# Speech joint training kernel: the two ge-row tiles are cleared by VectorE at the start instead of by GpSimd after the first chunk

## The chip, the core and the metric

The kernel runs on one core of a Trainium2 chip. The metric is device time in microseconds (us), the median of several executions. Three executions of the kernel before took 789.6, 789.79 and 791.91 us; the median is 789.79 us.

## What is computed

The reference is the forward pass of a small speech network with a joint layer, followed by the gradients of all seven inputs. The forward pass, with B = 2 sequences, T = 16000 time steps, D = 256 channels, K = 3 taps and U = 8 label steps, is:

```python
h = sum over i in 0..2 of xp[:, i:i+T] @ w1[i]        # x padded by one at both ends
h = gelu(h)[:, ::2]
f = sum over i in 0..2 of hp[:, i:i+T1] @ w2[i]       # h padded by one at both ends
f = gelu(f)[:, ::2]                                   # 4000 rows for each sequence
fe = f @ w_f
ge = g @ w_g                                          # 8 rows for each sequence
j  = tanh(fe[:, :, None, :] + ge[:, None, :, :])      # B, 4000, 8, 256
out = j @ w_o
```

The outputs are `out` and, from a given `grad_out`, the gradients with respect to x, w1, w2, g, w_f, w_g and w_o. All tensors are bf16.

## The kernel before, in words

**Tiling.** The 2 x 4000 rows of `f` are taken as one row of 8000 columns and cut into 17 chunks: one of 256 columns, fifteen of 512 and a last one of 64. Channels lie on the 128 partitions, two tiles (kt) for 256 channels. For each chunk `stage_a` loads x transposed (XC), runs the two convolutions with their gelus (HTo, HTe, FT; `conv_gelu`, whose operations stand at L514 to L539, also makes the gelu's derivative factors G1o, G1e and G2 on VectorE) and FE. `stage_j` then goes over the eight label steps in four pairs: it makes `tanh(fe + ge)` (JT), the output rows (OUT_SB), and the gradient that flows back into the tanh (NGZ, added up in ZS). `stage_de` takes the gradient of the chunk before back through the convolutions and adds up the weight gradients (ACC).

**The ge rows.** In most chunks VectorE makes the tanh's argument a second time, row-wise: `JR = FER + GEB` at L686, with the rows on the partitions. This needs the eight `ge` rows of a sequence on every partition, the tile GEB, 128 x 2048 bf16, one tile for each sequence. `make_geb` (L606) fills it: GpSimd clears the tile (`memset`, L609), four DMAs from the GpSimd queue put the 8 x 256 values of `ge` (GER) on partitions 0, 32, 64 and 96 (issued at L363), and VectorE's `stream_shuffle` (L615) copies each of the four rows to its group of 32 partitions. In the source the shuffle has a planned delay of 45 us (first sequence) or 100 us (second). `ge_rows` makes GER from gT and WG on TensorE, with an evacuation on VectorE (L351). The first chunks do not use GEB: chunks 0 and 1 get JR by transposing JT on TensorE.

**Order of the work.** Nothing is issued in the order of the source. Each operation is recorded with its engine or engines, a planned cost, what it reads and writes, and a due time; `Flow.issue` then plays a list schedule through with the planned costs and emits each engine's instructions in the order that it found. Some evacuations may go to ScalarE or VectorE, as the schedule decides. A change of one operation's engine or cost can thus change the order, and the engine, of others far behind it. All loads and stores but a few go through SyncE's queue.

**The start.** VectorE clears a small tile (L1043), TensorE runs 20 matmuls on it to be busy, ScalarE loads its table. SyncE issues the first XC load, the weights W2, WF and WOT, and three GO loads; GpSimd makes `ident` and issues the two GR loads, later the WG and WO loads. Then chunk 0 is convolved, `make_ge` makes GE (L1077 transposes GR against `ident`; L1089 evacuates), and stage_j of chunk 0 begins with JT (L654) and the transposes of JT (L681).

Inside `conv_gelu`, on VectorE: L520 makes `g_s` from `g_sq` and the PSUM tile of the convolution, and so frees that PSUM tile; L531, L533, L535, L537 and L539 follow, of which L535 and L537 are `tensor_scalar` operations on bf16 tiles in SBUF. ScalarE's L529 (tanh of `g_s`) waits for both L520 of a convolution. There are seven PSUM tiles (`ps`) that all stages share.

Of the kernel before, what the change touches and what calls it, by code (L numbers as in the profile page):

```python
# [10 lines left out]
BF16 = mybir.dt.bfloat16  # L11
# [25 lines left out]
class Flow:  # L37
# [24 lines left out]
    def buf(self, cls, shape, dtype, name):  # L62
        b = Buf(cls, shape, dtype, name)
        s = self.seq[cls]
        b.seq, s[0] = s[0], s[0] + 1
        return b

    def op(self, eng, cost, fn, r=(), w=(), new=(), at=None, work=0.0, after=(), kind=None, behind=(), sub=None, lag=0.0):
        o = Op()
        o.eng = (eng,) if isinstance(eng, str) else tuple(eng)  # L70
        o.cost = cost if isinstance(cost, tuple) else (cost,) * len(o.eng)
        o.fn, o.new, o.work, o.n = fn, list(new), work, len(self.ops)
        o.prio = ((self.now if at is None else at) + self.shift.get((self.stage, sub), 0.0), o.n)
        o.succ, o.done, o.ready, o.kind, o.span, o.lag = [], None, 0.0, kind, None, lag
        deps, bufs = set(after), []
        for lst, wr in ((r, False), (w, True)):
            for x in lst:
                b, key = x if isinstance(x, tuple) else (x, None)
                for d, k, dw in b.log:
                    if (wr or dw) and (k is None or key is None or k == key):  # L80
                        deps.add(d)
                if b not in bufs:
                    bufs.append(b)
        for lst, wr in ((r, False), (w, True)):
            for x in lst:
                b, key = x if isinstance(x, tuple) else (x, None)
                if wr:
                    b.log = [e for e in b.log if not (key is None or e[1] == key)]
                b.log.append((o, key, wr))
        for b in o.new:  # L90
            b.born = o
        deps.discard(o)
        o.soft = ({b.born for b in bufs if b.born is not None} | set(behind)) - deps - {o}
        deps |= o.soft
        for b in o.new:
            if b not in bufs:
                bufs.append(b)
        o.deps, o.bufs = deps, bufs
        for b in bufs:
            b.users += 1  # L100
        o.left = len(deps)
        for d in deps:
            d.succ.append(o)
        self.ops.append(o)
        return o
# [110 lines left out]
def c_dve(n, f=1.0):  # L216
    return 66.0 + 1.042 * n * f
# [3 lines left out]
def kernel(  # L221
# [19 lines left out]
    nc = tc.nc  # L241
    B, T, D = x.shape
    KK = w1.shape[0]
    U = g.shape[1]
# [6 lines left out]
    P = 128  # L251
# [43 lines left out]
    op, buf = F.op, F.buf  # L295
# [9 lines left out]
    def fixed(shape, dtype, name, pool=None):  # L305
        b = Buf(None, shape, dtype, name)
        b.t = (pool or const).tile(shape, dtype, name=name)
        return b
# [14 lines left out]
    GER = fixed([U, B, D], BF16, "GER")  # L323
# [33 lines left out]
    def dma(q, out, in_, r, w, bytes_, new=(), transpose=False, at=None, after=(), cost=None, behind=(), sub="dma"):  # L357
        def go(e):
            eng_ = nc.sync if e == "SP" else nc.gpsimd if e == "POOL" else nc.scalar
            if transpose:  # L360
                eng_.dma_start_transpose(out=out(), in_=in_())
            else:
                eng_.dma_start(out=out(), in_=in_())  # L363
        c = cost or (1230.0 if transpose else 750.0 if q == "POOL" else 450.0)
        return op(q, c, go, r=r, w=w, new=new, at=at, after=after, behind=behind, sub=sub, kind="T" if transpose else "D",
                  work=bytes_ / 32768 * 165.0 if transpose else bytes_ / 304.0)
# [238 lines left out]

    def make_geb(b):  # L606

        GEB = buf("geb", [P, U, D], BF16, "GEB")
        op("POOL", 2100.0, lambda e: nc.gpsimd.memset(GEB[:], 0.0), r=[(GER, b)], w=[GEB], new=[GEB])  # L609
        for q in range(0, P, 32):  # L610
            dma("POOL", lambda q=q: GEB[q:q + 1], lambda: GER[:, b, :], r=[(GER, b)], w=[(GEB, q)], bytes_=4096)

        def spread(e):
            v = GEB[:].rearrange("p u d -> p (u d)").bitcast(FP32)
            nc.vector.stream_shuffle(v, v, [0] * 32)  # L615
        op("DVE", 66.0 + c_dve(U * D // 2), spread, r=[GEB], w=[GEB], sub="geb", lag=45000.0 if b == 0 else 100000.0)
        return GEB

    def mix_geb(G0, G1):
        px = [c.px for c in chunks if c.px is not None][0]  # L620
        GEB = buf("gx", [P, U, D], BF16, "GEB")
        op("DVE", c_dve(U * D, 0.25), lambda e: nc.vector.tensor_copy(out=GEB[:], in_=G1[:]), r=[G1], w=[GEB], new=[GEB])
# [378 lines left out]
    def gg_out():  # L1001
# [43 lines left out]
       r=[(warm, 0)], w=[(warm, 1)])  # L1045
# [4 lines left out]
            mm(wps[:, 0:2 * P], warm[:, 0, 0], warm[:, 0].rearrange("p k c -> p (k c)"), True, True)  # L1050
    op("PE", 20 * 215.0, warm_up, r=[(warm, 0)], w=[wps], new=[wps])
    op("POOL", 500.0, lambda e: make_identity(nc, ident[:]), w=[ident])

    def wload(q, dst, out, in_, n, at, after=()):
        return dma(q, out, in_, r=[], w=[dst], bytes_=n * 65536, at=at, cost=450.0 if q != "POOL" else 550.0, after=after)
# [48 lines left out]
    GEB = GEBX = None  # L1104
    for k in range(NG + 1):
# [15 lines left out]
        if k + 1 < NG and chunks[k + 1].px is not None:  # L1121
            F.now = t0 + Wk * 0.3
            GEB1 = make_geb(1)
            GEBX = mix_geb(GEB, GEB1)
        if k == 1:
            F.now = t0 + Wk * 0.1
            ge_rows()
            GEB = make_geb(0)
# [3 lines left out]
        if k < NG and c.px is not None:  # L1132
            GEB = GEB1
# [43 lines left out]
```

## Time and profile before

| what | us |
|---|---|
| median of three executions | 789.79 |
| the profiled execution, own time | 789.48 |
| its span, first to last instruction | 787.7 |
| PE (TensorE) busy | 770.0 |
| ACT (ScalarE) busy | 725.5 |
| DVE (VectorE) busy | 714.1 |
| POOL (GpSimd) busy | 96.2 |
| the two clears of GEB on POOL, each | 1.80 |
| the two shuffles of GEB on DVE, each (78.7 and 147.5 us) | 1.31 |

How to read the answers of the trace: times are us from the span's start. A timeline line has the start, the duration of the merged group, the engine, the line of the kernel, the operation, the tiles written and read, the size, and, in square brackets, how long the engine had been idle before it and which instruction ended that. An engine with a "q" behind its name is its sequencer, which issues DMAs. In a table of waits, each line names who waited for whom, the total in us, how often, and the longest. A line of busy time by window has, for each engine, busy us and the number of instructions, then the TensorE clock that was granted as a share of full speed, the busy share of the DMA engines and GB/s.

### The profile page before, as it was taken

To read this page: it belongs to the slowest core of one execution; us is meant where nothing else is said; L and a number is where in the kernel's file an instruction comes from. 1 tells how busy PE (TensorE), PEld (TensorE's weight loads), DVE (VectorE), ACT (ScalarE), POOL (GpSimd) and SP (SyncE) were. 2 spreads that over 40 slices of the span, in tenths; PEclk is the share of its full clock that TensorE was granted. 3 is DMA by queue.
4 is the path that set the end of the run, shared out by engine and by line. 5 is a ranking of instruction groups with operands and counts; after the bars stand their busy time and mean duration, and the time that the engine had idled before them with its cause. 6 is when DMAs were issued, how large, how long until landed. Compare 5 with 4: busy or idle time off the path is not lost. (4 is left out here: it accounts for less than half of the span.)

```text
span 787.7 us, 15636 instructions
## 1 busy us (share of the span) xinstructions
PE 770.0 (98%) x5668; PEld 533.6 (68%) x5668; DVE 714.1 (91%) x1503; ACT 725.5 (92%) x1178; POOL 96.2 (12%) x235
## 2 busy tenths in 40 slices
PE   6999999999999999999999999999999999999997
PEld 4657767576675767767677666676767767577775
DVE  5799999998998989989899898998989899899965
ACT  4999989999999999999999999999999999999833
POOL 4311110201102010020101101010020110203010
PEclk8999999999999999999999999999999999999999
DMA  9998999999999999999999999999998989989984
GB/s 212 175 208 187 232 252 244 238 240 243 222 227 227 266 232 215 233 257 225 229 211 244 243 230 226 214 257 219 229 252 203 264 209 227 248 225 239 229 204 144
DMA packets 382754, 178.86 MB, mean 227 GB/s; under 512 B 307762, under 2 KB 376468, under 8 KB 380756
## 3 DMA queue, kind: packets, MB, share of 16 engines
q1 hardware_dynamic: 381122, 176.90, 100.2%
q8 instruction: 44, 0.72, 0.4%
q10 hardware_dynamic: 1138, 0.66, 0.3%
q0 software_dynamic: 416, 0.30, 0.1%
q14 instruction: 34, 0.28, 0.1%
HBM read 51.42 MB, written 50.34 MB: 129 GB/s over the span
## 5 line engine op out<-in xcount | busy, mean ns | idle before, releaser
L654 ACT ACTIVATE JT<-FE,GE 128x512 bf16<-128x512 bf16 (+4 forms) x288 | 185.2, 691 | 0.1
L739 DVE SCALAR_TENSOR_TENSOR NGZ<-JSQ,ps 128x512 f32<-128x512 bf16 (+3 forms) x252 | 149.9, 608 | 3.5 <-PE ps L337 3.2
L337 PE MATMUL ps<-WO,JT 128*128 128x256 bf16 x1000 | 149.1, 273 | 0.0
L337 PE MATMUL ps<-GOT,WOT 128*128 128x512 bf16 (+2 forms) x544 | 147.2, 363 | 0.1
L346 ACT CAST OUT_SB<-ps 128x512 bf16<-128x512 f32 (+1 forms) x215 | 129.0, 604 | 11.8 <-PE ps L337 11.7
L337 PEld LDWEIGHTS <-JT 128*128 128x128 bf16 x1000 | 97.7, 98 | 54.7 <-issue 0.2
L726 ACT ACTIVATE JSQ<-JT 128x1024 bf16<-128x1024 bf16 (+2 forms) x129 | 130.0, 1008 | 4.5 <-DVE NGZ L739 4.2
L337 PE MATMUL GWO<-GO,JR 128*128 128x256 bf16 x1000 | 130.0, 273 | 1.5 <-ACT JR L691 0.8
L691 ACT ACTIVATE JR<-JR 128x1024 bf16<-128x1024 bf16 x112 | 120.3, 1076 | 8.4 <-DVE JR L686 8.1
L756 DVE TENSOR_TENSOR ZS<-ZS,NGZ 128x1024 f32<-128x1024 f32 (+2 forms) x102 | 115.3, 1131 | 0.4
L337 PEld LDWEIGHTS <-JR 128*128 128x128 bf16 x1000 | 97.5, 98 | 17.8 <-ACT JR L691 1.5
L520 DVE SCALAR_TENSOR_TENSOR g_s<-g_sq,ps 128x512 bf16<-128x512 bf16 (+2 forms) x102 | 64.8, 638 | 39.9 <-ACT HTo L517 31.4
L337 PEld LDWEIGHTS <-W 128*128 128x128 bf16 x612 | 57.9, 98 | 59.9 <-issue 2.8
L337 PE MATMUL ps<-XC,W 128*128 128x512 bf16 (+2 forms) x408 | 84.5, 362 | 1.4 <-DMA XC<-in_x_dram 1.4
L337 PEld LDWEIGHTS <-X 128*128 128x128 bf16 (+1 forms) x756 | 73.8, 98 | 9.6
L686 DVE TENSOR_TENSOR JR<-FER,GEB 128x1024 bf16<-128x1024 bf16 x112 | 77.6, 697 | 1.5 <-PE GWO L337 1.0
L809 DVE TENSOR_TENSOR ACC<-ACC,ps 128x512 f32<-128x512 f32 x90 | 59.1, 679 | 18.1 <-PE ps L337 18.1
L337 PEld LDWEIGHTS <-WOT 128*128 128x128 bf16 x544 | 51.7, 98 | 21.6 <-issue 0.9
L348 ACT ACTIVATE GX_SB<-ps 128x512 bf16<-128x512 f32 (+1 forms) x107 | 63.3, 619 | 2.1 <-PE ps L337 1.8
L379 POOL COPY GF<-GF 128x254 bf16<-128x254 bf16 (+1 forms) x17 | 7.4, 435 | 469.4 <-issue 313.6
L514 ACT ACTIVATE g_sq<-ps 128x512 bf16<-128x512 f32 (+2 forms) x102 | 60.7, 595 | 1.0 <-PE ps L337 0.6
L337 PE MATMUL ps<-W1T,GHo 128*128 128x512 bf16 (+1 forms) x252 | 61.3, 326 | 0.0
(144 smaller groups left out, 1171.3 us busy)
## 6 DMA issues: line engine op xcount, KB each, us to landing
GO<-in_grad_out_dram SPq DMA_DIRECT2D x60, 512.0 KB, 5.5
out_dram<-OUT_SB SPq DMA_DIRECT2D x60, 512.0 KB, 6.7
X<-in_x_dram SPq DMA_DIRECT2D x15, 1088.0 KB, 7.1
out_dram<-GX_SB SPq DMA_DIRECT2D x30, 512.0 KB, 3.5
GOT<-GO SPq DMA_TRANSPOSE x65, 5.0
GO<-in_grad_out_dram SPq DMA_DIRECT2D x4, 256.0 KB, 4.8
out_dram<-OUT_SB SPq DMA_DIRECT2D x4, 256.0 KB, 3.6
XC<-in_x_dram SPq DMA_TRANSPOSE x62, 4.9
```

Of the source, the lines that this page charges most:

```text
L337: nc.tensor.matmul(ps_ap, lhsT=lhsT, rhs=rhs, start=start, stop=stop)
L346: nc.scalar.copy(out=dst(), in_=src())
L348: nc.scalar.activation(out=dst(), in_=src(), func=ACT.Copy, scale=scale)
L514: op("ACT", c_act(W, True), lambda e, mt=mt, ps=ps: nc.scalar.activation(out=sq[:, 0:A, mt, :Pw], in_=fl(ps[:, :W], A), func=ACT.Square, s ...
L520: op("DVE", c_dve(W), lambda e, mt=mt, ps=ps: nc.vector.scalar_tensor_tensor(out=s[:, 0:A, mt, :Pw], in0=sq[:, 0:A, mt, :Pw], scalar=1.0, ...
L654: nc.scalar.activation(out=fl(jtw(JT, j)[:, mt], A)[:, :, lo:hi], in_=FE[:, 0:A, mt, lo:hi], func=ACT.Tanh, bias=GE[:, b, mt, 2 * up + j:2 ...
L686: op("DVE", c_dve(n * 2 * D, 0.5), lambda e, lo=lo, n=n, m=m, JR=JR: nc.vector.tensor_tensor(out=JR[:m, 0:n], in0=S["FER"][:m, lo:lo + n]. ...
L691: op("ACT", c_act(n * 2 * D), lambda e, n=n, m=m, JR=JR: nc.scalar.activation(out=JR[:m, 0:n], in_=JR[:m, 0:n], func=ACT.Tanh), r=[JR], w= ...
L726: nc.scalar.activation(out=JSQ[:, :, :W], in_=jtw(JT, j), func=ACT.Square)
L739: nc.vector.scalar_tensor_tensor(out=fl(zap(), A)[:, :, lo:hi], in0=fl(JSQ[:, d2, :W], A)[:, :, lo:hi], scalar=1.0, in1=fl(ps[:, :W], A)[: ...
L756: nc.vector.tensor_tensor(out=a, in0=a, in1=b, op=ALU.add)
L809: op("DVE", c_dve(512), lambda e: nc.vector.tensor_tensor(out=acc_ap().rearrange("p k d -> p (k d)"), in0=acc_ap().rearrange("p k d -> p ( ...
```

## The change

The two GEB tiles are allocated at the start of the program, right behind the recording of `ident`, and cleared there by VectorE, as 1024 words of 32 bits per partition. `make_geb` takes the tile of its sequence from the list, and keeps its four DMAs and the shuffle.

```diff
     def make_geb(b):
-        GEB = buf("geb", [P, U, D], BF16, "GEB")
-        op("POOL", 2100.0, lambda e: nc.gpsimd.memset(GEB[:], 0.0), r=[(GER, b)], w=[GEB], new=[GEB])
+        GEB = GEB01[b]
         for q in range(0, P, 32):
             dma("POOL", lambda q=q: GEB[q:q + 1], lambda: GER[:, b, :], r=[(GER, b)], w=[(GEB, q)], bytes_=4096)
...
     op("POOL", 500.0, lambda e: make_identity(nc, ident[:]), w=[ident])
+    GEB01 = []
+    for b in range(B):
+        GZ = buf("geb", [P, U, D], BF16, "GEB")
+        op("DVE", 650.0, lambda e, GZ=GZ: nc.vector.memset(GZ[:].rearrange("p u d -> p (u d)").bitcast(mybir.dt.uint32), 0), w=[GZ], new=[GZ])
+        GEB01.append(GZ)
```

The two programs' instruction orders, set side by side, differ as follows. GpSimd loses the two clears, and its eight GEB DMAs stand in one row ahead of the XC copies of chunk 1, where before two of the eight stood among those copies. VectorE gets the two clears as its second and third instruction. SyncE's order is the same. The first shuffle of GEB stands seven VectorE instructions earlier (near 74 us of the profile before), the second twenty instructions earlier (near 135 us). Between about 135 and 186 us VectorE and ScalarE run the same work in another order, and two evacuations go from VectorE to ScalarE; TensorE has two swaps of neighbouring groups of matmuls there, and is the same in all else.

## The prediction

> **What bounds the kernel now.** I read the page's busy times and slices first, then the waits of TensorE, then the timeline at the place of the change.
>
> ```profile
> PE 770.0 (98%) x5668; PEld 533.6 (68%) x5668; DVE 714.1 (91%) x1503; ACT 725.5 (92%) x1178; POOL 96.2 (12%) x235
> ...
> PE   6999999999999999999999999999999999999997
> ```
>
> TensorE is busy for 770.0 of 787.7 us, and the first slice (0 to 20 us) is the only early one below 9. The waits of TensorE after 48 us (the view of waits, PE alone, 48 us to the end) are few:
>
> ```profile
> PE ps L337 <- DVE NGFE L753: 0.9, 1, 0.9
> PE GWO L337 <- ACT JR L691: 0.8, 2, 0.6
> PE GWO L337 <- ACT JR L346: 0.4, 1, 0.4
> ```
>
> With three smaller ones (0.3, 0.2, 0.2) they add up to 2.8 us in 740, and none is on a DMA. So the end comes when TensorE has done its row of work: time won before 48 us is won at the end, unless the new order makes TensorE wait later.
>
> The timeline from 11 to 18 us shows what the clears do (all engines; only the rows that matter):
>
> ```profile
> 10.35 0.28 DVE L537 TENSOR_SCALAR g_s<-g_s 128x512 bf16<-128x512 bf16 x1
> ...
> 11.88 3.54 POOL L609 MEMSET GEB<- 128x2048 bf16 x2
> ...
> 12.11 3.46 DVE L537 TENSOR_SCALAR g_s<-g_s 128x512 bf16<-128x512 bf16 x1
> ...
> 13.06 0.37 ACT L346 CAST FE<-ps 128x256 bf16<-128x256 f32 x1 [0.19 <-PE ps L337]
> ...
> 13.30 0.24 PE L337 MATMUL ps<-gT,WG 128*128 128x8 bf16 x4
> ...
> 15.49 0.27 DVE L535 TENSOR_SCALAR g_sq<-g_sq 128x512 bf16<-128x512 bf16 x1
> ...
> 16.15 1.25 PE L337 MATMUL ps<-WG,gT 128*8 128x256 bf16 x4 [2.60 <-DVE g_s L520]
> ...
> 16.80 0.63 ACT L529 ACTIVATE g_s<-g_s 128x512 bf16<-128x512 bf16 x1 [3.36 <-DVE g_s L520]
> ...
> 17.33 2.09 ACT L654 ACTIVATE JT<-FE,GE 128x256 bf16<-128x256 bf16 x5
> ...
> 17.88 1.91 PE L681 MATMUL psb<-ident,JT 128*128 128x128 bf16 x8 [0.48 <-ACT JT L654]
> ```
>
> The same VectorE instruction, in the same shape, took 0.28 us at 10.35 and 3.46 us at 12.11; the long one began under the two GpSimd clears (11.88 to 15.42) and ended 0.15 us behind them. Behind it TensorE waited 2.60 us and ScalarE 3.36 us, both for VectorE's L520. The clears are not on the path by their own result (the shuffle comes at 78.7 us), but by what they hold up.
>
> **Part 1: the clears leave GpSimd.** L537 falls back to 0.28 us: 3.46 - 0.28 = 3.18 us. Its successor on VectorE, L535, starts 0.2 us after the start of L537 in undisturbed pairs (10.35 after 10.14, in the other order), so at 12.3 in place of 15.49: all of VectorE's work moves by **3.17 us**. What comes late next? L520's inputs are there (ScalarE's g_sq ended at 12.32 and 12.87). ScalarE is free at 13.43, so L529 can go from 16.80 to 13.63 and JT from 17.33 to 14.16. TensorE is at 13.54 when the WG,gT matmuls come; their wait goes. The next wait, for JT at 17.88, moves to 14.71. From here on TensorE, ScalarE and VectorE wait for one another in the same way, 3.17 us earlier. What does not move is the XC load of chunk 1: its last part is in at 24.37 (GpSimd's copy L407 was released by it then), and the convolution that needs it started at 28.95, now 25.78: 1.4 us of cover. The GO load at 22.95 was released by TensorE's GWO group, and SyncE was free at 21.67; the third GOT tile has to be there at 34.13, now 30.96, and was issued at 19.81 with 4.6 us to landing in this stretch. So the whole 3.17 us passes.
>
> **Part 2: the clock.** TensorE was granted half its clock in two windows:
>
> ```profile
> 14.78:18.19 3.41, 1.45 (x5) 0.40 (x4) 3.41 (x12) 1.40 (x4) 0.65 (x1) 0.50 0.92 165
> 18.19:21.60 3.41, 3.10 (x17) 2.17 (x18) 2.82 (x10) 3.07 (x8) 1.80 (x4) 0.50 1.12 160
> 11.37:14.78 3.41, 0.97 (x15) 0.84 (x13) 3.38 (x4) 1.87 (x6) 3.27 (x4) 1.00 1.16 208
> 7.95:11.37 3.42, 3.08 (x33) 2.60 (x33) 3.12 (x12) 2.65 (x9) 0.98 (x3) 1.00 1.03 301
> ```
>
> Behind a window with 0.97 us of matmuls the clock fell, behind one with 3.10 it came back. After the change the window to 14.78 gains only some 0.4 us of matmuls (the WG,gT group, 1.25 us at half clock), so I take it that the clock still falls. The next window then holds the work that gave 3.10 us, and the clock is back at 18.19, where the shifted work of before had it at 21.60 - 3.17 = 18.43. That is 0.24 us of matmuls at full instead of half speed: **0.12 us**.
>
> **Part 3: the clears on VectorE.** The nearest row is the clear of the small tile, 128x128 words in 0.17 us at 0.83. Eight times as many words cost 1.36 us at most, 2.7 us for two; as cheap as a copy of the same bytes (L622, 128x2048 bf16, 0.68 us) they are 1.4. I take 2.7, the row of the same operation. They run from 1.0 to 3.7 us, behind the small clear that TensorE's first matmuls wait for. VectorE's next work is at 8.03, behind 7.03 us of idle time, and waits for ScalarE. They cost **nothing**; without that cover, up to 2.7.
>
> **Part 4: what else moves.** The eight GEB DMAs (0.52 us each) start when GER is there, 16.6 in place of 19.80, and end by 20.8, ahead of the copy L407 at 24.37, which has to wait for its load. The copy L413 behind it loses one DMA in front of it. Cost nothing. The two shuffles (1.31 us each, DVE) stand 7 and 20 instructions earlier, and 135 to 186 us has another order. At worst both shuffles come between TensorE and its PSUM tiles: 2 x 1.31 = 2.6 us lost; at best a wait goes that is there, and TensorE has none from 91 to 467 us: nothing to gain. I take **0**: before, the same shuffles stood in the same dense stretch and TensorE did not wait. Both ends stay in the range.
>
> Sum: 3.17 + 0.12 = 3.3 us. The profiled execution goes from 789.48 (span 787.7 and 1.8 around it) to 786.2, the span to 784.4; the median shown lies 0.3 above the profiled one, so **786.5 us**.
>
> **The rivals.**
>
> *A. The clock does not fall.* If 0.4 us more of matmuls keep it up, TensorE is no longer late for ScalarE's evacuations at 20.68 and 22.09 (waits of 0.34 and 0.41 in the timeline), and ScalarE, which is full from 24 to 30, sets the rest: 3.17 + 0.75 = 3.9, 785.9 us. Against it: the window is still nearer to 0.97 than to the 2.02 of 4.54 to 7.95, which kept the clock.
>
> *B. The clock stays at half to 21.60.* The work now starts at 14.71, so 3.17 us more of it run at half speed, 1.6 us lost: 788.2 us. [...]
>
> *C. The clears on VectorE hold up GpSimd,* as the clears on GpSimd held up VectorE: `ident` and the GR loads (issued at 1.49 and 2.13, landing some 4.5 later, 6.65) come 2.7 us later, at 9.3; TensorE needs them at 7.89, so 1.4 us lost, 787.9 us. [...]
>
> *D. One bad cluster from the new order.* Between 45.49 and 48.07, where the pairs of chunk 1 begin, TensorE waited 0.56, 0.13, 0.70 and 0.36 for ScalarE and VectorE: 1.75 us. One such place in the new order: 788.2 us.
>
> *E. Slower: the new order does not fit.* From 130 to 180 us TensorE, ScalarE and VectorE were busy for 50.00, 49.68 and 49.33 of 50 us, so there is no slack to take a worse order. The stretch of 51 us that changes is about one chunk, four pairs; a cluster of 1.75 us in each is 7.0, less 3.3: 3.7 us slower, 793.5 us. It decides once TensorE's waits after 48 us pass 2.8 + 3.3 = 6.1. Against it: the same planner with the same costs left 0.8 us of waits in the 420 us from 48 to 468.
>
> *F. The change does not do what it says:* L537 stays long because something else than the clears holds it, 789.8 us. The ends within 0.15 us speak against it.
>
> **How the numbers follow.** Forecast 0.53, A 0.10, B 0.08, C 0.06, D 0.12, E 0.09, F 0.02. A measurement of this kernel can tell about 0.3% from no change, 2.4 us, so the border is at 787.4: faster is the forecast and A, 0.63; the same is B, C, D and F, 0.28; slower is E, 0.09. The range 785.3 to 789.0 takes in the forecast, A to D, reaches 0.6 below A for other early waits of TensorE that may go (0.32 at 28.07, 0.50 at 36.99), and leaves out E and F.
>
> **What would show it.** Right: no VectorE L537 over 0.5 us before 20 us; JT's first instruction near 14.2; the half clock ending near 18.2; chunk 1's convolution starting near 25.7; TensorE's busy time as before (near 770 less 0.5), its waits after 48 us near 2.8. Wrong: TensorE's start at 6.49 or the GR transposes at 7.89 later (C), half clock to 21.6 (B), waits between 135 and 190 us (D, E), or a wait on XC at 25 us.

## The result, and the profile after

The changed kernel took 787.13 us (median of nine executions, 785.95 to 789.47) against 789.79 us before (nine executions, 789.43 to 792.01). The ratio is 0.996, with a 95% interval of 0.9946 to 0.9974: 2.7 us less by the medians, a small gain, but the interval leaves out 1. The profiled execution took 785.95 us, with a span of 784.2 us against 787.7. That is 3.5 us less, and it is the fastest of the nine.

The page of the changed kernel, to be held against the first lines of the prediction:

```profile
PE 766.7 (98%) x5637; PEld 532.5 (68%) x5668; DVE 711.2 (91%) x1503; ACT 726.3 (93%) x1180; POOL 93.4 (12%) x233
...
PE   7999999999999999999999999999999999999996
```

TensorE (PE) still sets the end. The same stretch of the timeline as before, with the rows that answer to those shown there:

```profile
1.16 0.91 DVE L1055 MEMSET GEB<- 128x1024 uint32 x1 [0.16 <-issue]
...
2.24 0.91 DVE L1055 MEMSET GEB<- 128x1024 uint32 x1 [0.16 <-issue]
...
12.12 0.28 DVE L537 TENSOR_SCALAR g_s<-g_s 128x512 bf16<-128x512 bf16 x1
...
13.48 0.60 PE L337 MATMUL ps<-WG,gT 128*8 128x256 bf16 x4
...
13.63 0.63 ACT L529 ACTIVATE g_s<-g_s 128x512 bf16<-128x512 bf16 x1 [0.19 <-DVE g_s L520]
...
14.16 2.09 ACT L653 ACTIVATE JT<-FE,GE 128x256 bf16<-128x256 bf16 x5
...
14.71 0.23 PE L680 MATMUL psb<-ident,JT 128*128 128x128 bf16 x1 [0.63 <-ACT JT L653]
```

L537, 3.46 us before, takes 0.28 us. TensorE's wait of 2.60 us ahead of the WG,gT matmuls is gone, and ScalarE's JT starts at 14.16 in place of 17.33. The two clears lie far from any other VectorE work.

The granted clock in the two windows that were at 0.50 before (busy time by window; the column behind POOL is the clock):

```profile
14.78:18.19 3.41, 2.90 (x27) 2.30 (x28) 3.30 (x13) 3.41 (x9) 1.86 (x4) 1.00 0.85 148
18.19:21.60 3.41, 3.41 (x38) 3.10 (x36) 3.09 (x12) 3.41 (x9) 2.28 (x5) 1.00 1.15 161
```

In this execution the clock doesn't fall before the last 2 us (at 782.27 of 784.2). The same TensorE row at the start of the next chunk, the first convolution over XC, came at 28.95 before and comes here:

```profile
23.87 0.77 PEld L337 LDWEIGHTS <-JR 128*128 128x128 bf16 x8 [0.77 <-ACT JR L346]
23.87 1.05 PE L337 MATMUL GWO<-GO,JR 128*128 128x256 bf16 x8 [0.49 <-DMA XC<-in_x_dram]
...
24.75 2.54 PE L337 MATMUL ps<-XC,W 128*128 128x512 bf16 x11
```

That is 4.20 us earlier: 3.17 from the stall, and 1.03 more in the stretch whose clock had been at half. (The bracket at 23.87 names the XC load, but these matmuls do not read XC; their weight load waited for ScalarE's JR, as the row above says, and so I put the 0.49 us down to JR.) I then followed the same TensorE rows through both traces. The lead is 4.18 us at chunk 2 (96 us of before), 3.90 at chunk 3 (145), 3.84 at chunk 4 and 3.73 at chunk 5 (242), and stays at 3.72 to 3.73 up to 771 us. So 0.45 us were given back between 96 and 242 us, most of it where the planner's order is new, and another 0.2 us at the very end, behind VectorE's last row.

### The profile page after: what moved, and what is told of

It is laid out like the page before. It is cut to its first block, busy times and chain, and to the rows that moved or that the text cites. A ratio compares the mean times of both kernels' runs of the same rounds, so it can differ in the third digit from the quotient of the medians.

```text
span 784.2 us, 15603 instructions
## 1 busy us (share of the span) xinstructions
PE 766.7 (98%) x5637; PEld 532.5 (68%) x5668; DVE 711.2 (91%) x1503; ACT 726.3 (93%) x1180; POOL 93.4 (12%) x233
## 5 line engine op out<-in xcount | busy, mean ns | idle before, releaser
L346 ACT CAST OUT_SB<-ps 128x512 bf16<-128x512 f32 (+1 forms) x219 | 130.9, 603 | 9.6 <-PE ps L337 9.5
L348 ACT ACTIVATE GX_SB<-ps 128x512 bf16<-128x512 f32 (+1 forms) x104 | 61.6, 620 | 2.1 <-PE ps L337 1.8
L337 PE MATMUL ps<-GHoR,X 128*128 128x256 bf16 (+1 forms) x378 | 57.7, 273 | 0.0
```

Source lines behind the costliest of these rows:

```text
L337: nc.tensor.matmul(ps_ap, lhsT=lhsT, rhs=rhs, start=start, stop=stop)
L346: nc.scalar.copy(out=dst(), in_=src())
L348: nc.scalar.activation(out=dst(), in_=src(), func=ACT.Copy, scale=scale)
```

## The experiments

Two theories stood against each other. **The block:** a GpSimd clear holds a VectorE instruction of L537's kind for as long as it lasts, and whatever removes the overlap gains. **The order:** the planner's new order is what gains, or the clears have to be on VectorE. A third question came with the spread of the nine executions: what the clock adds. All ten kernels were timed beside the kernel before, whose median in these runs was 790.7 to 791.5 us.

### The clears on VectorE, but in the old order

```diff
+    def clears(e):
+        nc.vector.memset(warm[:, 0], 0.0)
+        for b in range(B):
+            nc.vector.memset(GEB01[b][:].rearrange("p u d -> p (u d)").bitcast(mybir.dt.uint32), 0)
-    op("DVE", 200.0, lambda e: nc.vector.memset(warm[:, 0], 0.0), w=[(warm, 0)], new=[warm])
+    op("DVE", 200.0, clears, w=[(warm, 0)], new=[warm])
...
-        op("POOL", 2100.0, lambda e: nc.gpsimd.memset(GEB[:], 0.0), r=[(GER, b)], w=[GEB], new=[GEB])
+        op("POOL", 2100.0, lambda e: None, r=[(GER, b)], w=[GEB])
```

> The clears run on VectorE right behind the small clear at the start, but every other instruction stands exactly where it stood before the change: the planner still sees the old clears. Theory (the GpSimd clears blocked VectorE's L537 for 3.18 us, and the new order costs 0.45 us between 134 and 241 us): L537 is 0.28 us, TensorE starts chunk 1's convolution near 24.75, and this shift of 4.2 us stays whole from there on, so the best executions end 0.3 to 0.5 us earlier than those of the changed kernel, 785.5. Rival (the new order is what gains, not the clears): no shift, 789.8.

Measured: 788.3 us median (787.02 to 789.42), ratio 0.9959 (0.9947 to 0.9971). The order is not what gains: with the old one, JT starts at 14.36. The lead over the kernel before, 2.88 us at chunk 1, is still 2.84 at chunk 2 and 2.83 at chunk 5, so the old order gives nothing back. But the forecast of the time is a miss by 1.5 us and more. In all five executions the granted clock was below 0.999, and in the profiled one a window fell to half again:

```profile
15.48:18.89 3.41, 3.13 (x18) 2.28 (x18) 2.82 (x9) 2.88 (x7) 2.36 (x5) 0.50 1.29 137
```

The lead at chunk 1 is 2.88 us in place of 4.20. Of these 1.3 us, 0.20 are there before: the first XC load landed later, and TensorE's first convolution started at 6.69 in place of 6.49. The other 1.12 us come between JT and chunk 1's convolution, and are the price of the window.

### GpSimd clears early

The two GpSimd clears are issued right behind the second GR load; the old order otherwise.

```diff
+        if b == B - 1:
+            o.fn = lambda e, go=o.fn: (go(e), [nc.gpsimd.memset(G[:], 0.0) for G in GEB01])
```

> GpSimd does both clears as before the change, but behind the GR loads, from about 2.7 to 6.2 us, while VectorE has nothing to do; no other instruction moves. Theory (it matters only that no VectorE instruction of the blocked kind runs beside the clears, not which engine clears): L537 0.28 us, same gain as with the clears on VectorE in the old order, 785.5 to 787. Rival (GpSimd is then late for the XC copy at 6.5, or the clears have to be on VectorE): less than half of the gain, over 788.

Measured: 786.75 us median (785.56 to 790.82), ratio 0.9941 (0.9928 to 0.9954). GpSimd cleared from 2.64 to 6.21 us, while VectorE was idle, and both early L537 took 0.28 to 0.29 us. From L537 to JT there are 2.05 us (13.96 to 16.01), 5.22 before and 2.04 in the changed kernel. The gain is there, by the median, without any clear on VectorE. So what matters is when the clears run, not which engine does them. The profiled execution itself is the slowest of the five (790.82) and shows no lead at chunk 1 (-0.21 us): its first XC load landed at 7.08, its clock rose only at 9.88, and it was at half again from 16.71 to 23.53 and from 47.43 to 50.84.

### The clears on GpSimd, in place, but held until GER is there

```diff
+        def clear(e):
+            nc.gpsimd.tensor_copy(out=GEB[0:U, 0, 0:1], in_=GER[:, b, 0:1])
+            nc.gpsimd.memset(GEB[:], 0.0)
-        op("POOL", 2100.0, lambda e: nc.gpsimd.memset(GEB[:], 0.0), r=[(GER, b)], w=[GEB], new=[GEB])
+        op("POOL", 2100.0, clear, r=[(GER, b)], w=[GEB], new=[GEB])
```

> The clears stay on GpSimd in their old place, but a copy of one column of GER stands ahead of each, so that they wait for GER, as the planner had assumed, and run from about 16.1 to 20.0 us, beside VectorE work without tensor_scalar or copies from SBUF to SBUF. No other instruction moves. Theory: nothing is blocked, 785.5 to 787, although GpSimd does more work than before. Rival (any VectorE work beside a GpSimd clear is slowed): a VectorE instruction of over 1.5 us near 16 to 20 us, and 788.5 or more.

Measured: 788.15 us median (785.61 to 788.99), ratio 0.9952 (0.9936 to 0.9967). The best two executions, at a clock of 0.999, took 785.61 and 785.63. The median is above the forecast; the other four had a clock of 0.993 to 0.997. The profiled execution is the slowest (788.99): the stall is gone, JT starts at 14.34, and then the clock is at half from 14.74 to 21.57, two windows long:

```profile
14.70:18.20 3.50, 2.98 (x16) 2.00 (x17) 2.91 (x10) 3.16 (x9) 1.87 (x2) 0.51 1.07 169
18.20:21.60 3.40, 3.40 (x18) 2.40 (x17) 1.27 (x6) 2.67 (x7) 3.34 (x6) 0.50 1.02 150
```

This run also shows what ran wrong in the kernel before. The planner had placed the clears behind GER, but a clear reads nothing, so no wait held it there, and GpSimd ran it as soon as it came to it, at 11.88. With a real wait, in the timeline of this kernel, it runs beside other VectorE work without harm:

```profile
16.65 1.80 POOL L611 MEMSET GEB<- 128x2048 bf16 x1
16.83 0.69 DVE L351 COPY JR<-psb 128x1024 bf16<-128x1024 bf16 x1
...
18.63 1.81 POOL L611 MEMSET GEB<- 128x2048 bf16 x1
...
19.08 0.43 DVE L731 TENSOR_TENSOR JSQ<-JT 128x512 bf16<-128x512 bf16 x1
```

A copy out of PSUM (0.69 us) and a `tensor_tensor` (0.43 us) under the clears take what they take elsewhere (0.67 to 0.69 and 0.42 to 0.43). L537, a `tensor_scalar` from SBUF to SBUF, did not get through in the kernel before: 3.46 us beside the clears, where it takes 0.28 without them. Why it was held and the other two were not, no run shows.

### The changed kernel with the GpSimd clears put back

```diff
+            if T_ is st[0]["G1o"]:
+                F.ops[-1].fn = lambda e, go=F.ops[-1].fn: (go(e), [nc.gpsimd.memset(G[:], 0.0) for G in GEB01])
```

> The changed kernel with both GpSimd clears put back behind the first chunk's G1o, a second time over the same tiles; the order is that of the changed kernel. Theory: L537 is 3.4 to 3.5 us again, TensorE waits 2.6 us, the clock falls again, and the whole gain goes: 789.8 to 790.7 (the new order's 0.45 us remains). Rival (order): no loss against the changed kernel, 786 to 787.

Measured: 792.49 us median (790.55 to 793.43), ratio to the kernel before 1.0015 (1.0004 to 1.0025): above the forecast. The whole gain goes and 1.2 us more. In the profiled execution 0.47 us of it is lost between 96 and 242 us, the new order's, and 0.36 behind VectorE's last row, where the trace gives no reason; the rest isn't assigned. The stall is back in the same form:

```profile
13.84 3.54 POOL L384 MEMSET GEB<- 128x2048 bf16 x2
14.07 3.46 DVE L539 TENSOR_SCALAR g_s<-g_s 128x512 bf16<-128x512 bf16 x1
...
18.11 1.25 PE L337 MATMUL ps<-WG,gT 128*8 128x256 bf16 x4 [2.60 <-DVE g_s L522]
```

### Half of each clear

GpSimd clears the second half of each tile in the old place and order, VectorE the first half at the start.

```diff
+        op("POOL", 2100.0, lambda e: nc.gpsimd.memset(GEB[:, U // 2:], 0.0), r=[(GER, b)], w=[GEB])
```

> The order of before; GpSimd clears only the second half of each tile in the old place (2 x 0.9 us), VectorE the first half at the start. Theory (a blocked VectorE instruction waits for as long as the GpSimd clears last): L537 ends some 0.15 us behind the clears, near 13.8, so 1.7 us in place of 3.46; JT starts near 15.6 (17.33 before, 14.16 to 14.36 without clears); of the 3.17 us 1.8 are won, 788.0 to 789.5 as the clock falls. Rival (VectorE is held by a fixed cost for each of the two clears, or for its own reasons): L537 again near 3.4 us.

Measured: 788.68 us median (788.15 to 790.56), ratio 0.9979 (0.997 to 0.9988).

```profile
13.75 1.84 POOL L610 MEMSET GEB<- 128x1024 bf16 x2
13.97 1.76 DVE L538 TENSOR_SCALAR g_s<-g_s 128x512 bf16<-128x512 bf16 x1
...
17.49 0.89 ACT L655 ACTIVATE JT<-FE,GE 128x256 bf16<-128x256 bf16 x2
```

Half the clear, half the block. The instruction ends at 15.73, 0.14 us behind the clears; in the kernel before it was 0.15, with the clears put back 0.15. The start of chunk 0's work is 1.9 us late in this execution because the clock rose late (its first twelve matmuls over XC took 2.72 us in place of 1.47; more below), so the distance is what counts: from L537 to JT there are 3.52 us here, 5.22 before and 2.04 after the change.

### The kernel before, with TensorE kept busy in the gap

```diff
-                for kt in range(KT):
+                for kt in [0, 1] * (11 if c.first and mt else 0) + [0, 1]:
                     mm(fl(ps[:, :W], A), WF[:, kt, mt * P:(mt + 1) * P], FT[:, 0:A, kt, :Pw], kt == 0, kt == KT - 1)
...
-                for mt in range(KT):
+                for mt in [0, 1] * (4 if b == 0 else 0) + [0, 1]:
```

> The kernel before, with TensorE repeating the second FE product of chunk 0 eleven times and the first small GE product four times into the same PSUM tiles, so that it is busy from 13 to 15.5 us and in part from 11.3 to 12.6; the stall of VectorE stays. Theory (the gain has a second part, the clock: each half-clock window of 3.4 us early on costs 1.2 to 1.3 us): L537 3.46 us and JT at 17.3 as before, but no half clock from 14.8 to 21.6, and 1.0 to 1.3 us less than before in the same session (791.15), 789.9. Rival (the clock is only a symptom of the stall): no difference from before.

Measured: 789.82 us median (788.31 to 791.9), ratio 0.9988 (0.9977 to 0.9999). The profiled execution has the stall and no half clock:

```profile
11.97 3.46 DVE L537 TENSOR_SCALAR g_s<-g_s 128x512 bf16<-128x512 bf16 x1
12.50 3.00 PE L337 MATMUL ps<-FT,WF 128*128 128x256 bf16 x26 [0.74 <-ACT FT L517]
```

It starts chunk 1 only 1.17 us earlier than the kernel before. Of these, 0.14 are there before the stall, as the first XC load landed earlier (6.34 against 6.49); from JT to chunk 1's convolution there are 10.59 us, just as in the changed kernel, and 11.62 before. So the clock's part is 1.03 us, and apart from the stall's 3.17. By the medians it is 0.9 us, a little under the forecast; eight of eleven executions were still granted only 0.996 or 0.997.

### The changed kernel with the gaps filled

The same small GE fill, and the second GER product repeated three times.

```diff
-                for kt in range(KT):
+                for kt in [0, 1] * (3 if b == 1 else 0) + [0, 1]:
                     mm(ps[:U, 0:D], gT[b][:, kt, :], WG[:, kt, :], kt == 0, kt == KT - 1)
```

> The changed kernel, with TensorE repeating the first small GE product four times and the second GER product three times into the same PSUM tiles, in the gaps before 12.6 and before 14.7 us. Theory (the spread of the changed kernel, 785.95 to 789.47, is half-clock windows that come or not by where the clock's windows lie; granted clock 0.999, 0.997 and 0.992): the clock falls in fewer executions, median nearer to 786 than to 787.13. Rival (the spread has another source): same median and spread as the changed kernel, 787 and up.

Measured: 787.83 us median (786.16 to 788.33), ratio 0.9962 (0.9947 to 0.9976): a miss. All six executions were granted 0.999, as forecast, and still four took 787.68 to 788.33. So there was a second source, which the clock column does not show. A candidate stands in profiles of the runs above. In the run with the clears put back, the first convolution of chunk 0 took 2.72 us for twelve matmuls, against 1.47 in the changed kernel:

```profile
1.06 4.45 PE L337 MATMUL ps<-g_sq 128*128 128x256 bf16 x20 [1.06 <-DVE g_sq L1044]
6.81 2.72 PE L337 MATMUL ps<-XC,W 128*128 128x256 bf16 x12 [1.31 <-DMA XC<-in_x_dram]
```

The first clock record of that trace, a rise to full, is at 10.46 us; in the changed kernel's it is at 4.03. The page gives 1.00 for all time before the first record, but the matmuls there take 1.85 times as long (2.72 against 1.47 us). That those four executions are of this kind no trace shows, as the one that was profiled took 786.62 us; the runs with more matmuls at the start speak to it.

### Old order, gaps filled, and 26 matmuls at the start

```diff
-        for _ in range(20):
+        for _ in range(26):
```

> The clears on VectorE in the old order, with the fills of the run before, and 26 matmuls at the start in place of 20, so that TensorE also is busy up to about 5.5 to 6.5 us. Theory: no half clock in most executions; 785.3 to 786.0 median, the fastest of all. Rival: no better than the clears in the old order alone, 787 to 788.

Measured: 785.79 us median (785.56 to 786.89), ratio 0.994 (0.9927 to 0.9953). It has the lowest median, and its spread is 1.3 us where the changed kernel had 3.5. TensorE's idle time ahead of the first convolution is 0.77 us in place of 1.65, and the lead at chunk 1, 4.29 us, is still 4.27 at chunk 5. The first convolution starts when the first XC load has landed, and that alone lay between 6.33 us (here) and 7.08 us in the profiled executions, so part of every lead is chance.

### The same in the new order

> The changed kernel with both fills and 26 matmuls at the start: it differs from the fastest run so far (785.79, the clears in the old order with the same fills) by the planner's new order alone. Theory (the new order costs 0.45 us between 134 and 241 us): 786.2, with the clock at 0.999 in most executions; in the profile the shift against the kernel before falls from 4.2 us to 3.7 between 134 and 241 us. Rival (the order is free): 785.8.

Measured: 786.34 us median (786.01 to 787.83), ratio 0.9943 (0.9926 to 0.9959). Its median is 0.55 us above that of the run before it, but the two were timed in different sessions, and against the kernel before beside them the ratios are alike. The traces decide: the lead over the kernel before falls from 4.03 us at chunk 2 to 3.52 at chunk 5. In the four profiled executions in the new order this loss is 0.44 to 0.51 us, in the seven others in the old order at most 0.02. The new order costs half a microsecond. Two of its pieces in the changed kernel are starts of TensorE rows that lie 349 and 361 ns apart at 134 and 138 us, where 216 is usual. The view of waits has them as no idle time at all, since the row of a 512-column matmul, 0.38 us long, covers them.

This is also the changed kernel with the gaps filled, with six more matmuls at the start. Without them, four of six executions took 787.7 us or more at a clock of 0.999; here none at 0.999 is above 786.4. That supports the late rise of the clock as the second source, though no execution of that group was profiled.

### The kernel before with 26 matmuls at the start

> The kernel before with 26 matmuls at the start in place of 20, nothing else. Theory (the kernel before has two groups of times, 789.4 to 790.2 and 791 to 792.3, because in some executions the clock comes up at 4.5 us and in others, where TensorE's idle 1.4 us before 6.5 spoils a window, only near 10.4): only the lower group remains, median 789.6, while the stall and the two half-clock windows behind it stay. Rival (the two groups have another source): both groups again, median 790.5 to 791.

Measured: 790.31 us median (789.86 to 791.72), against 791.46 for the kernel before beside it; ratio 0.9992 (0.9983 to 1.0001), which can't be told from no change. But ten of fifteen executions of the kernel before took 791.1 us or more, and one of eleven here: the upper group all but goes. The median is 0.7 above the forecast, and why is open. In the profiled execution (790.75) the 26 matmuls end at 6.75, and the first convolution starts at 6.93, when the XC load has landed, 0.44 us later than before; the matmuls did not hold it up there.

## Why the prediction was right, step by step

The forecast was 786.5 us, and 787.13 was measured. The stall was understood; that the number came out so near owes something to luck, as the last lines of this part say.

- **Part 1, the stall: right.** Forecast 3.17 us; JT moved from 17.33 to 14.16. That it fits to the hundredth is luck: the first XC load landed at 6.49 in both profiled executions, and elsewhere between 6.33 and 7.08. Clears early, held, halved or put back all behave as the block says. The cover held too: the XC load of chunk 1 landed at 24.5, before the convolution at 24.75. It was closer than the 1.4 us that I gave it, because TensorE came a further 1.0 us earlier.
- **Part 2, the clock: the term that was mis-sized.** I took 0.12 us and let the clock fall. In the profiled execution it did not fall, which was rival A; it brought 1.03 us (A had 0.75). The step that failed was to leave the clock's windows where they had lain before. In these two traces the clock's changes lie whole multiples of 3.413 us behind its rise (before: rise at 4.54, changes at 14.78 and 21.60; after: rise at 4.03, the next change at 782.27, 228 of them later), so I count the windows from the rise. Here the clock rose at 4.03 in place of 4.54, so the window ahead of the dip ran from 10.86 to 14.27 and held 2.19 us of matmuls, where the one before had 0.97. With one window at half, as forecast, the run with the old order shows what comes: a lead of 2.88 us, or 3.08 without its later load, against the sum's 3.29. What I missed is that this is drawn anew in each execution: the rise came at 4.03, 4.54, 9.88 and 10.46 in four profiled ones (changed kernel, before, early clears, clears put back). Three of nine took 785.95 to 786.1 at a clock of 0.999, five 787.11 to 788.89 at 0.997, which by my count is one window (half of 3.41 us in 785 is 0.002), and one 789.47 at 0.992, which is three; where these windows lay was not recorded. The median therefore lies between A's 785.9 and B's 788.2, above the forecast. The late rise of the clock in some executions, which fits the two groups of the kernel before, was in none of my cases.
- **Rival B:** not in the execution of the changed kernel that is shown, where the window from 14.27 to 17.69 held all eight transposes of JT (L680) and 1.5 us of other matmuls and kept the clock at 1.00. But B's two windows at half did come, without any stall, in the profiled executions with early and with held GpSimd clears. Their first windows, 16.71 to 20.12 and 14.74 to 18.16, had 3.02 and 2.94 us of matmuls, 1.86 and 1.57 without the transposes, and the clock stayed down. It came back behind windows with 3.10 us (2.02 without) in the kernel before, and 3.13 (2.28) in the old order. Both counts put these four windows in the same order, so the runs don't settle which of them goes with the clock. Nor is the fall a matter of TensorE's busy time in the window alone: a window with 2.06 us of matmuls (42.05 to 45.46, held clears) was followed by half clock, one with 1.56 (4.41 to 7.83, gaps filled) was not.
- **Part 3, the clears: right** in that they cost nothing. Two rows of 0.91 us, 1.08 apart, end at 3.15, under the bound of 1.36 each; VectorE's next work comes at 8.04. **Rival C** fell: GpSimd's `ident` (0.29 us at 1.02) and the GR issues (1.16 us for two) beside them were as before (0.29 us at 1.01, and 1.16). The five stalls in the traces end 0.13 to 0.15 us behind the second clear, and in the four with whole clears L537 was held over two of them in a row, for 3.46 us.
- **Part 4, the new order: inside the stated ends, but not nothing.** I took 0, with up to 2.6 lost at worst; it costs 0.44 to 0.51 us. **Rivals D and E** asked for clusters of 1.75 us, and there is none; TensorE's waits after 48 us are 2.4 us, 2.8 before. **F** fell with L537.
- **The tail.** The profiled span shows 0.2 us less gain than the rows at 771 us; other runs have -0.1 to 0.45 there. VectorE's last row still ends 3.72 us earlier (783.84 before, 780.12 after); from there to the end of the span, while the last stores go out, there are 3.86 us before and 4.05 after, 3.74 to 4.30 in the other runs. So no row of work is in it. No experiment was made on it, and what makes it longer stays open.

The sum for the profiled execution: 3.17 + 1.03 - 0.45 - 0.2 = 3.5 us, against the forecast's 3.3. The clock brought 0.91 us more than I took, the order and the tail cost 0.65 that I did not count, and these errors largely cancel.

## What to carry to other kernels

An instruction off the path can hold the path (here L537 took 3.46 us in place of 0.28): look for one row that takes many times its usual duration, and for what runs on GpSimd at that moment. A planned place is not a wait: the clear, which read nothing, ran as soon as GpSimd came to it (11.88 us, against 16.65 with a real wait), so give such an instruction a place where its neighbours don't mind, or something real to wait for. Where a kernel's executions spread by more than the effect, compare the same row in both traces, and hold TensorE's clock steady first: in the new order, the fills and the six matmuls narrowed the spread from 3.5 us (nine executions) to 1.8 (five).

## What the runs showed of the hardware

- Two GpSimd clears of 1.80 us, one behind the other, held one `tensor_scalar` for both: it took 3.46 us in place of 0.28 and did not get in between them. A copy out of PSUM and a `tensor_tensor` ran beside such clears at their usual 0.69 and 0.43 us.
- Half-clock stretches were 3.41 us long (old order, 15.48 to 18.89) or 6.83 (before, 14.78 to 21.60), but for the one at the end of each trace. From JT to chunk 1's convolution there were 10.59 to 10.67 us in the five profiled executions without one there, 11.71 with one full window (old order) and 13.01 and 13.15 with two (held and early clears): 1.1 to 1.3 us for a window that TensorE would have filled. They can also come at 45 to 51 us, behind TensorE's waits between two chunks: in the run with held clears the lead fell there from 1.60 to 0.43 us.
- The page's granted clock reads 1.00 before the trace's first clock record, even where twelve matmuls take 2.72 us instead of 1.47 (the run with the clears put back).
